# First tokens turned inside the routing steps, two whole weight quarters fetched ahead of them, row numbers written during the dense layers

## The chip, the cores and the metric

The kernel runs on one NeuronCore of a Trainium2 chip. A core has TensorE (PE: matmuls; PEld: its weight loads), VectorE (DVE), ScalarE (ACT), GpSimd (POOL) and SyncE (SP). Each takes its instructions in the order of the program and waits for semaphores of the others. Sixteen DMA engines move data between HBM and the on-chip memory; here SP issues nearly all transfers and POOL the gathers and the final scatter, which go by lists of row numbers. The metric is the device time of one execution in microseconds (us).

## The reference

Three stages, one behind the other, all in float32:

```python
x = attention(q, k, v)      # 2 x 8 heads x 768 x 64: a window of 16 on each side, and 24 block summaries
logits = x @ w_gate         # [1536, 8]
for idx in argsort(-logits.flatten()):          # greedy: the best (token, expert) pair first
    if token free and expert has fewer than 192 tokens: assign
out[mask_e] = relu(x[mask_e] @ w1[e]) @ w2[e]   # 8 experts of 192 tokens, 512 -> 1024 -> 512
h = out @ w_in; g = where(h >= 1, h, where(h <= -1, 0, (h + 1)**2 / 4))
result = g @ w_out          # 512 -> 2048 -> 512
```

## The kernel before

**Attention** (lines 103 to 404) is a list of small steps, written out by hand in ORDER (lines 53 to 100); each step issues on a fixed engine, so the list is the order of every engine's queue. Its last steps are `x_turn` (four transposes of 128 finished tokens, line 346), `x_out` (their copy out of PSUM), `logits` (eight matmuls with `w_gate`, line 357), `logits_out` (their copy into `lg`, line 130 on DVE) and `x_store` (the tokens to the DRAM tensor `xdram`, line 341).

**Routing** finds the greedy assignment in eight phases, one for each expert that fills. `scale` (line 478) reduces `lg` to its largest magnitude `m`, spreads it over the partitions with a transpose and a matmul (lines 484, 489), and finds with `best` (lines 506 to 514, five DVE operations) each token's best expert `oh`. A phase then makes five rounds (`first`, `mask`): DVE writes a mask `mk` (line 677), PE counts with twelve matmuls (line 565), DVE makes flags, PE spreads them with one matmul (line 575). PE and DVE take turns here, and each waits for the other. At the end of a phase the chosen expert's number `ei` is known (the step `expert`), and some steps on, its 192 row numbers `idx` (line 688, the step `places`).

**Experts.** `fetch` (line 711) gathers the 192 tokens of an expert in two halves of 96 rows (line 717, on POOL), and stores the row numbers to the DRAM tensor `idxd` (line 719, on SP). For the first expert SP also issues a tiny store `spare` of one gathered row (line 723): SP waits there until the second half has landed, and all later weight loads stand behind it. An expert's weights come as four quarters of 1 MB (`weights`, line 725): two of w1, two of w2. The first quarter of the first expert is cut in two halves (lines 744, 745), of which one stands ahead of the tokens. `transposed` (line 749) turns one half of the tokens on PE and copies it out on ACT; `mlp` (line 760) is a generator of 64 steps of one matmul each (lines 776, 785).

**What sets the order.** `run_experts` runs the routing generator; PLAN gives, for each of its turns, how much PE work of another kind is put in. While `turns` (counted from the first `places` on) is at most WAIT = 8, that is `idle(n)`: n matmuls on zeros (line 709) that compute nothing. After that it is n steps of the experts' products. The first of these turns both halves of the first tokens (`turn(0)`, with three idle matmuls ahead of each half).

**Dense layers.** `FeedForward.steps` makes 16 rounds (`s`) of seven products, takes weights as 64-bit `raw` tiles from SP, which DVE converts, and scatters results to rows `idxo`, which `run` reads back from `idxd` (line 1208) at its start.

**Pools.** Tiles come from pools. A pool opened on bytes of closed pools makes its tiles wait, by default, for every user of those pools, transfers included.

Of the kernel before, what the change touches and what calls it, by code (L numbers as in the profile page):

```python
# [36 lines left out]
2 5 2 1 2 2 2 2 2 2 2 2 2 1 10 10 3 3 3 3 3 2 4 2 2 2 2 9 9 2 3 3 3 3 3 3 3 3 2 2 16 9 3 3 3 3 3 3 3 3 3 2 2 10  # L37
# [3 lines left out]
WAIT = 8  # L41
# [56 lines left out]
logits_out 8 act; x_store 11; x_turn 11; pv_out 9 1; x_out 11 dve; x_turn 9; x_store 9; x_out 9 act; logits 11;  # L98
logits 9; logits_out 11 dve; logits_out 9 dve
# [3 lines left out]
def attention(tc, ctx, C, q, k, v, wg, xdram, lg, later, order=ORDER):  # L103
# [239 lines left out]
    def x_turn(t):  # L343
        p = live["xp", t] = ptr()
        for c in range(4):
            nc.tensor.transpose(p[:, c], live["x", t][:, c * 128:(c + 1) * 128], ident)  # L346
# [5 lines left out]
    def logits(t):  # L352
        p = live["l", t] = ptr()
        for c in range(4):
# [7 lines left out]
    def begin():  # L362
        warm = st.tile([128, 512], BF, name="warm")
# [43 lines left out]
class Router:  # L407
# [15 lines left out]
    def open(self, ctx):  # L423
        self.wk = ctx.enter_context(self.tc.tile_pool(name="rt_work", bufs=2, side="right"))
        self.pp = ctx.enter_context(self.tc.tile_pool(name="rt_psum", bufs=2, space=PSUM, side="right"))

    def consts(self):
# [27 lines left out]
        g.memset(self.ones, 1.0)  # L455
# [21 lines left out]

    def scale(self):
# [14 lines left out]
        r = wk.tile([128, 2], F32, name="r")  # L493
        nc.vector.tensor_scalar(r[:, 0:1], p[:, :1], 1.0 / (half - 0.25), 1e-36, op0=OP.mult, op1=OP.max)
        nc.vector.reciprocal(r[:, 1:2], r[:, 0:1])

        self.v0 = wk.tile([128, NT], F32, name="v0")
        nc.vector.tensor_scalar(self.v0, v, r[:, 1:2], half, op0=OP.mult, op1=OP.add)
        self.r = r
# [18 lines left out]
    def phase(self, k):  # L518
# [13 lines left out]
        if not last:  # L532
            oh = self.oh
            for j in range(LEVELS):
# [25 lines left out]
                if k == 0 and j == 0:  # L560
                    nc.vector.tensor_scalar(Z, self.lg, self.r[:, 1:2], KARY / 2, op0=OP.mult, op1=OP.add)
# [129 lines left out]
class Experts:  # L691


    def __init__(self, tc, ctx, C, xdram, w1, w2, router, ff, idxd, spare, xp):
        self.tc, self.nc, self.C, self.spare = tc, tc.nc, C, spare
        self.x, self.w1, self.w2, self.rt = xdram, w1, w2, router
        self.ff, self.idxd, self.xp = ff, idxd, xp
        self.quarters = 0
        self.post = []
        self.wk = ctx.enter_context(tc.tile_pool(name="ex_work", bufs=2))  # L700
        self.pp = ctx.enter_context(tc.tile_pool(name="ex_psum", bufs=2, space=PSUM))
# [9 lines left out]
    def fetch(self, k):  # L711
# [13 lines left out]
    def weights(self, k, j, q):  # L725
# [16 lines left out]
        if k == 0 and j == 0:  # L742

            q.dma_start(a[:, :, :256], src[:, :, :256])
            self.rest = lambda: q.dma_start(a[:, :, 256:], src[:, :, 256:])
        else:
            q.dma_start(a, src)
# [49 lines left out]
def run_experts(router, ex, ff, leave, plan=PLAN):  # L797
# [26 lines left out]
    def load():  # L824

        while loaded[0] < min(4 * known[0], room() if placed[0] else 1):
            k, j = divmod(loaded[0], 4)

            if loaded[0] == 1:
                ex.rest()  # L830
# [35 lines left out]
    for r in route():  # L866
# [10 lines left out]
        else:  # L877
            ex.idle(n)
    for n, _ in enumerate(run):
# [5 lines left out]
class FeedForward:  # L885
# [7 lines left out]
    def __init__(self, tc, ctx, C, w_in, w_out, idxd, out):  # L893
        self.tc, self.nc, self.ctx = tc, tc.nc, ctx
        self.w_in, self.w_out, self.idxd, self.out = w_in, w_out, idxd, out
# [202 lines left out]
    def early(self, spare):  # L1098

        nc, tc = self.nc, self.tc  # L1100
        self.wk = self.ctx.enter_context(tc.tile_pool(name="ff_work", bufs=2, side="right"))
        self.pp = self.ctx.enter_context(tc.tile_pool(name="ff_psum", bufs=2, space=PSUM, side="right"))
# [21 lines left out]
    def steps(self):  # L1124
# [74 lines left out]

    def run(self, ctx):  # L1200
        nc, tc = self.nc, self.tc
        self.ww = ctx.enter_context(tc.tile_pool(name="ff_split", bufs=3))
        self.op = ctx.enter_context(tc.tile_pool(name="ff_out", bufs=1, space=PSUM))
# [3 lines left out]
        idx = self.idx = self.st.tile([128, NT], I32, name="idxo")  # L1207
        nc.sync.dma_start(idx, bass.AP(tensor=self.idxd.tensor, offset=self.idxd.offset, ap=[[1, 128], [128, NT]]))
# [4 lines left out]
def build(tc, q, k, v, w_gate, w1, w2, w_in, w_out, out):  # L1213
    nc = tc.nc
    with ExitStack() as ctx:
# [17 lines left out]
        with ExitStack() as c1:  # L1233
            attention(tc, c1, C, q, k, v, wg, xdram, lg, (rt.consts, rt.consts2))
        ff = FeedForward(tc, ctx, C, w_in, w_out, idxd, out)
        c4 = ExitStack()
        xp = c4.enter_context(tc.tile_pool(name="ex_x", bufs=2, side="right"))
# [32 lines left out]
```

## Time and profile before

| | |
|---|---|
| median of the runs shown | 597.09 us (593.78, 597.09, 1673.16) |
| the profiled execution | 594.48 us |
| its span on the core | 592.4 us |
| PE busy | 569.9 us (96%) |
| DVE, ACT, POOL busy | 405.1, 276.4, 174.3 us |
| chain that ended last: PE, DVE, issue | 82%, 10%, 2% |

The 2.1 us between span and execution lie outside the core's instructions. In forty slices PE is at 9 tenths or more nearly everywhere from slice 9 on; slices 6 and 7 (89 to 118 us) hold the passage from attention to the experts. Busy there includes the idle matmuls on zeros, so the busy share alone does not show what work is done.

### The profile page before, as it was taken

Reading aid. Unit: us, or ns where it says so; the run is one execution under the profiler, and the core shown is the slowest. Engines: PE = TensorE matmul, PEld = TensorE weight load, DVE = VectorE, ACT = ScalarE, POOL = GpSimd, SP = SyncE. Lnnn points to the kernel's source line nnn. Section 1 sums busy time; section 2 is a strip of 40 time slices with the busy share of each in tenths; the row PEclk is TensorE's granted clock in tenths of the full one; section 3 lists DMA queues with packets and bytes.
Section 4 is the critical chain, followed back from the end, with each engine's and each line's share of the span. In section 5 each row is a group of like instructions: output and inputs, shape, how many; then the busy total and the mean of one; then the engine's idle time right before and its main releaser. Section 6 shows DMA issues by size and latency. Waiting matters only on the chain.

```text
span 592.4 us, 11433 instructions
## 1 busy us (share of the span) xinstructions
PE 569.9 (96%) x4298; PEld 485.2 (82%) x4298; DVE 405.1 (68%) x1092; ACT 276.4 (47%) x637; POOL 174.3 (29%) x271
## 2 busy tenths in 40 slices
PE   6799998999999999999999999999999999999996
PEld 4568683478988888899999988888888888989884
DVE  6887775753665755645666898886799886666651
ACT  5576670021222222223221756566677766666653
POOL 5412100100101101113000443333355875555424
PEclk9999998999999999999999999999999999999999
DMA  9999124388738659598888232100000100000002
GB/s 214 189 207 203 38 75 143 52 284 286 231 114 280 208 108 282 108 189 221 286 284 279 88 102 89 37 2 1 1 0 1 71 37 2 0 1 1 2 0 107
DMA packets 84073, 71.42 MB, mean 121 GB/s; under 512 B 42546, under 2 KB 71218, under 8 KB 84018
## 3 DMA queue, kind: packets, MB, share of 16 engines
q1 hardware_dynamic: 81506, 64.38, 39.8%
q0 software_dynamic: 1984, 6.29, 4.2%
q8 instruction: 34, 0.56, 0.4%
q14 instruction: 21, 0.17, 0.1%
q10 hardware_dynamic: 528, 0.02, 0.1%
HBM read 64.38 MB, written 6.30 MB: 119 GB/s over the span
## 4 chain that ended last, share of the span: by engine, by line
PE 82%; DVE 10%; issue 2%; ACT 2%; POOL 1%; DMA 1%; POOLq 0%; DVEq 0%; SPq 0%
PE po L1049 18%; PE ph L1016 17%; PE acc L776 15%; PE acc L785 14%; PE rt L565 2%; PE po L318 2%; PE pt L304 2%; PE px L709 2%; PE ps L280 1%; PE ptr L212 1%; DVE gl L1032 1%; DMA nat<-in_q_dram 1%; PE px L757 1%; PE ptr L346 1%; POOL out_dram L1067 1%
## 5 line engine op out<-in xcount | busy, mean ns | idle before, releaser
L776 PE MATMUL acc<-xt,slot 128*128 128x192 f32 x512 | 94.3, 333 | 0.6 <-ACT xt L758 0.6
L785 PE MATMUL acc<-ht,slot 128*128 128x192 f32 x512 | 94.2, 332 | 0.0
L776 PEld LDWEIGHTS acc<-xt,slot 128*128 128x128 f32 x512 | 82.3, 190 | 1.3 <-ACT xt L758 0.8
L785 PEld LDWEIGHTS acc<-ht,slot 128*128 128x128 f32 x512 | 82.5, 190 | 0.5
L994 POOL TENSOR_TENSOR al<-sums,ah 128x256 fp32r<-128x256 f32 x64 | 52.8, 827 | 89.4 <-ACT ah L993 79.9
L1016 PE MATMUL ph<-yh,ah 128*128 128x384 f32 x218 | 75.1, 344 | 1.7 <-DVE c L1119 1.1
L1049 PE MATMUL po<-wl,gh 128*128 128x512 f32 x192 | 76.0, 396 | 0.3 <-POOL wl L1007 0.3
L1049 PE MATMUL po<-wh,gl 128*128 128x512 f32 x192 | 75.9, 395 | 0.0
L1049 PE MATMUL po<-wh,gh 128*128 128x512 f32 x192 | 75.8, 395 | 0.0
L1016 PE MATMUL ph<-yl,ah 128*128 128x384 f32 x218 | 73.7, 338 | 0.0
L1016 PE MATMUL ph<-yh,al 128*128 128x384 f32 x218 | 73.6, 338 | 0.0
L717 POOL DMA_INDIRECT xg<-xdram,idx x16 | 15.0, 937 | 179.9 <-ACT idx L688 59.5
L994 POOL TENSOR_TENSOR al<-slot,ah 128x256 fp32r<-128x256 f32 x48 | 41.6, 867 | 79.0 <-PE ph L1016 43.0
L1029 ACT ACTIVATE gh<-u 128x384 fp32r<-128x384 f32 x64 | 33.4, 522 | 59.0 <-DVE u L1027 58.6
L1032 DVE TENSOR_TENSOR gl<-u,gh 128x384 fp32r<-128x384 f32 x64 | 51.3, 801 | 6.8 <-ACT gh L1029 6.7
L780 ACT ACTIVATE ht<-acc 128x192 f32<-128x192 f32 x64 | 21.0, 330 | 64.0 <-PE acc L776 64.0
L1016 PEld LDWEIGHTS ph<-yh,ah 128*128 128x128 f32 x218 | 40.9, 188 | 9.9 <-DVE u L1146 3.0
L1016 PEld LDWEIGHTS ph<-yl,ah 128*128 128x128 f32 x218 | 40.9, 188 | 3.9
L1049 PEld LDWEIGHTS po<-wl,gh 128*128 128x128 f32 x192 | 36.1, 188 | 6.1 <-POOL wl L1007 0.7
L1049 PEld LDWEIGHTS po<-wh,gl 128*128 128x128 f32 x192 | 36.1, 188 | 6.0
L1016 PEld LDWEIGHTS ph<-yh,al 128*128 128x128 f32 x218 | 40.9, 188 | 0.0
L790 ACT ACTIVATE yr<-acc 128x192 f32<-128x192 f32 x32 | 10.5, 330 | 64.5 <-PE acc L785 64.5
(228 smaller groups left out, 996.0 us busy)
## 6 DMA issues: line engine op xcount, KB each, us to landing
slot<-in_moe_w_dram SPq DMA_DIRECT2D x31, 1024.0 KB, 8.3
raw<-in_moe_w_in_dram SPq DMA_DIRECT2D x16, 512.0 KB, 5.4
raw<-in_moe_w_out_dram SPq DMA_DIRECT2D x16, 512.0 KB, 5.4
vw<-in_v_dram SPq DMA_DIRECT2D x20, 192.0 KB, 5.7
nat<-in_k_dram SPq DMA_DIRECT2D x12, 256.0 KB, 5.0
nat<-in_q_dram SPq DMA_DIRECT2D x12, 256.0 KB, 5.3
xdram<-xs SPq DMA_DIRECT2D x12, 256.0 KB, 2.9
slot<-in_moe_w_dram SPq DMA_DIRECT2D x2, 512.0 KB, 5.6
```

What stands on the lines that cost most here:

```text
L304: nc.tensor.transpose(pt[:, c], pr[:, c], ident)
L318: nc.tensor.matmul(po[64 * w:64 * w + 64, c], pt[:, c, 64 * w:64 * w + 64], VW[b * G + i // 2][:, n, 2 * c + a], start=True, stop=True)
L565: nc.tensor.matmul(p[:KARY, :E], mk[:, t], oh[:, t], start=(t == 0), stop=(t == NT - 1))
L717: nc.gpsimd.indirect_dma_start(out=self.XG[k][:, h], out_offset=None, in_=self.x, in_offset=bass.IndirectOffsetOnAxis(ap=idx[:, h:h + 1], ...
L776: nc.tensor.matmul(p, w[:, c, f % 4 * 128:f % 4 * 128 + 128], xt[:, c], start=(c == 0), stop=(c == 3))
L780: nc.scalar.activation(ht[:, f], p, AF.Relu)
L785: nc.tensor.matmul(p, w[:, f, c % 2 * 128:c % 2 * 128 + 128], ht[:, f], start=(f == 0), stop=(f == 7))
L994: nc.gpsimd.tensor_tensor(l, x, h.bitcast(F32), op=OP.subtract)
L1016: nc.tensor.matmul(p, w[:, 128 * c:128 * c + 128], y[:, b, c], start=first and n == 0, stop=n == 5, skip_group_check=True)
L1029: nc.scalar.activation(gh, u, AF.Copy)
L1032: nc.vector.tensor_tensor(gl, u, gh.bitcast(F32), op=OP.subtract)
L1049: nc.tensor.matmul(self.po[t], x[:, c], w, start=(self.left[t] == 6 * self.PAIRS - 1), stop=(self.left[t] == 0))
```

## The change

1. `reuse_waits="tile"` on the pools that are opened after attention (routing, experts, dense work): a tile waits only for earlier users of its own bytes.
2. `scale` is split: for the first 8 of 12 token tiles the five operations of `best` run inside attention's list (`later 2`), for the last 4 between the steps of `scale`; the scaling by a constant goes into the matmul (`ones` holds it, `tiny` keeps the sum above zero), so one DVE operation falls away.
3. Four matmuls on zeros (`unread`) in the last `x_turn` and `logits` steps.
4. Two whole quarters of the first expert's weights are loaded ahead of the `spare` store; the cut quarter is gone.
5. The two halves of the first tokens are turned at routing turns 5 and 6 (HALVES), without the idle matmuls; WAIT is 7, and PLAN is changed to suit.
6. The eight stores of row numbers leave `fetch`; a new `rows` issues them, and the read of `idxo`, in round 5 of the dense layers.

```diff
 PLAN = """
-2 5 2 1 2 2 2 2 2 2 2 2 2 1 10 10 3 3 3 3 3 2 4 2 2 2 2 9 9 2 3 3 3 3 3 3 3 3 2 2 16 9 3 3 3 3 3 3 3 3 3 2 2 10
+3 2 3 2 1 2 2 2 2 2 2 2 2 2 1 10 10 3 3 3 2 2 2 3 2 2 2 2 9 9 2 3 3 3 3 3 3 3 3 2 2 16 9 3 3 3 3 3 3 3 3 3 2 2 10
...
-WAIT = 8
+WAIT = 7
+HALVES = 5, 6
...
-logits_out 8 act; x_store 11; x_turn 11; pv_out 9 1; x_out 11 dve; x_turn 9; x_store 9; x_out 9 act; logits 11;
-logits 9; logits_out 11 dve; logits_out 9 dve
+logits_out 8 act; x_store 11; x_turn 11 1; pv_out 9 1; x_out 11 dve; later 2; x_turn 9 2; x_store 9; x_out 9 act; logits 11;
+logits 9 1; logits_out 11 dve; logits_out 9 dve
...
+    def unread(p, n):
+        for _ in range(n):
+            nc.tensor.matmul(p.rearrange("p a b -> p (a b)"), live["warm"][:, :128], live["warm"], start=True, stop=True)
...
-        self.wk = ctx.enter_context(self.tc.tile_pool(name="rt_work", bufs=2, side="right"))
+        self.wk = ctx.enter_context(self.tc.tile_pool(name="rt_work", bufs=2, side="right", reuse_waits="tile"))
...
     def scale(self):
 
         nc, wk, lg = self.nc, self.wk, self.lg
+        rest = list(self.first(slice(8, NT)))
         m = wk.tile([128, 1], F32, name="m")
         nc.vector.tensor_reduce(m, lg, axis=AX.XY, op=OP.max, apply_absolute_value=True)
+        yield "scale"
         p = self.ps()
         nc.tensor.transpose(p[:1, :128], m, self.C["ident"])
+        for o in rest[:2]:
+            o()
         yield "scale"
         m2 = wk.tile([1, 1], F32, name="m2")
         nc.vector.tensor_reduce(m2, p[:1, :128], axis=AX.X, op=OP.max)
         p = self.ps()
-        nc.tensor.matmul(p[:, :1], self.ones[:1], m2, start=True, stop=True)
+        nc.tensor.matmul(p[:, :1], self.ones, self.tiny, start=True, stop=False)
+        nc.tensor.matmul(p[:, :1], self.ones, m2, start=False, stop=True)
         yield "scale"
-        v = yield from self.best(lg)
+        for o in rest[2:]:
+            o()
...
-        nc.sync.dma_start(bass.AP(tensor=self.idxd.tensor, offset=self.idxd.offset + k // 4 * (N // 2) + k % 4 * 96,
-                                  ap=[[1, 96], [HALF, 2]]), idx)
...
-        while loaded[0] < min(4 * known[0], room() if placed[0] else 1):
+        while loaded[0] < min(4 * known[0], room() if placed[0] else 2):
...
-    def turn(k):
-        for h in range(2):
-            if k == 0:
-                ex.idle(3)
+    def turn(k, halves=(0, 1)):
+        for h in halves:
             ex.transposed(k, h)
-        turned[0] = k + 1
+        turned[0] = k + (halves[-1] == 1)
...
             ex.idle(n)
+            if turns in HALVES:
+                turn(0, (HALVES.index(turns),))
...
+            if s == P - 3:
+                self.rows()
...
+    def rows(self):
+
+        nc, d = self.nc, self.idxd
+        for k in range(E):
+            nc.sync.dma_start(bass.AP(tensor=d.tensor, offset=d.offset + k // 4 * (N // 2) + k % 4 * 96,
+                                      ap=[[1, 96], [HALF, 2]]), self.places[k])
+        self.idx = self.st.tile([128, NT], I32, name="idxo")
+        nc.sync.dma_start(self.idx, bass.AP(tensor=d.tensor, offset=d.offset, ap=[[1, 128], [128, NT]]))
```

How the change moves instructions is shown at three places. First DVE, from the last copies of `lg` to the first mask `mk`, before:

```order
L130 COPY xt<-ptr 128x512
L130 COPY lg<-ptr 128x8 x2
L482 TENSOR_REDUCE m<-lg 128x1
L487 TENSOR_REDUCE m_1712<-rt 1x1
L506 TENSOR_REDUCE v<-lg 128x12
...
L514 TENSOR_TENSOR oh<-w,mx 128x96
L494 TENSOR_SCALAR r<-rt 128x1
L495 RECIPROCAL r<-r 128x1
L498 TENSOR_SCALAR v_1734<-v,r 128x12
L540 TENSOR_SCALAR zi<-v_1734 128x24
L677 TENSOR_TENSOR mk<-zi,lev_500 128x384
```

and now:

```order
L131 COPY xt<-ptr 128x512
L501 TENSOR_REDUCE v0b<-lg 128x8
...
L131 COPY lg<-ptr 128x8 x2
L512 TENSOR_REDUCE m<-lg 128x1
L501 TENSOR_REDUCE v0b<-lg 128x4
L502 TENSOR_TENSOR w_1634<-lg,v0b 128x32
L520 TENSOR_REDUCE m_1733<-rt 1x1
...
L505 TENSOR_TENSOR oh_1636<-w_1634,mx_1635 128x32
L529 RECIPROCAL r<-rt 128x1
L532 TENSOR_SCALAR v_1747<-v0b,r 128x12
L574 TENSOR_SCALAR zi<-v_1747 128x24
L711 TENSOR_TENSOR mk<-zi,lev_500 128x384
```

Five operations on eight tiles of tokens stand ahead of the copies of `lg` now, two on the other four tiles between `m` and the maximum over partitions, three behind it, and one step of the scaling is gone.

Second PE, in the first expert's wait for its tokens (the second phase of the routing), before, from the flags of its fourth round on:

```order
L575 MATMUL rt<-fl,unit_508 128x2
L709 LDWEIGHTS blank
L709 MATMUL px<-blank 128x512
...
L757 MATMUL px<-ident,xg 128x96 x4
...
L757 MATMUL px<-ident,xg 128x96 x4
L776 MATMUL acc<-xt,slot_1671 128x192 x2
L565 LDWEIGHTS mk
L565 MATMUL rt<-oh,mk 32x8
```

and now, from the flags of its second round to its fourth count:

```order
L609 MATMUL rt<-fl,unit_506 128x2
...
L784 MATMUL px<-ident,xg 128x96 x4
L599 LDWEIGHTS mk
L599 MATMUL rt<-oh,mk 32x8
...
L784 MATMUL px<-ident,xg 128x96 x4
L609 MATMUL rt<-fl,unit_507 128x2
...
L599 MATMUL rt<-oh,mk 32x8
L803 MATMUL acc<-xt,slot_1686 128x192 x3
```

The first half of the tokens (`xg`) is turned ahead of the third count, the second half ahead of the third round's flags, and the first product (`acc`) follows the fourth count; before, both halves and the first product stood between the fourth flags and the fifth count.

Third SP's queue around the first tokens (`slot` is a weight quarter, `spare` the store that waits for the tokens, `ISA` sets an address), before:

```order
L729 TENSOR_LOAD ei
L729 ISA x2
L744 ISA
L744 DMA slot_1671<-in_moe_w_dram 128x4x256
L719 DMA idxd<-idx_1990 96x2x1
L723 DMA spare<-xg 1x8
L745 ISA
L745 DMA slot_1671<-in_moe_w_dram 128x4x256
L747 ISA
L747 DMA slot_1672<-in_moe_w_dram 128x4x512
```

and now:

```order
L761 TENSOR_LOAD ei
L761 ISA x2
L774 ISA
L774 DMA slot_1686<-in_moe_w_dram 128x4x512
L774 ISA
L774 DMA slot_1687<-in_moe_w_dram 128x4x512
L755 DMA spare<-xg 1x8
L774 ISA
L774 DMA slot_1688<-in_moe_w_dram 128x8x256
```

Ahead of the tokens stand 2 MB instead of half a megabyte, and the store of the row numbers is gone from between.

## Rows read from the trace of the kernel before

**Rows 1.** Stretches: length, then PE, PEld, DVE, ACT, POOL busy; clock, DMA, GB/s.

```profile
145.00:330.00 185.00, 183.19 (x1364) 170.04 (x1363) 111.78 (x427) 47.38 (x133) 19.20 (x23) 1.00 0.72 210
330.00:350.00 20.00, 19.09 (x103) 17.31 (x102) 18.48 (x30) 11.23 (x28) 9.20 (x9) 1.00 0.37 106
```

**Rows 2.** Timeline, end of attention to first count: start, length, what [idle before <-releaser].

```profile
92.02 0.17 DVE L130 COPY lg<-ptr 128x8 f32<-128x8 f32 x1 [0.65 <-PE ptr L357]
92.63 0.25 DVE L482 TENSOR_REDUCE m<-lg 128x1 f32<-128x96 f32 x1 [0.45 <-DMA xdram<-xs]
93.63 0.38 PE L489 MATMUL rt<-m,ones 1*128 1x1 f32 x2
93.94 1.68 PE L709 MATMUL px<-blank 128*128 128x512 bf16 x7
94.66 0.26 DVE L514 TENSOR_TENSOR oh<-w,mx 128x96 bf16<-128x96 bf16 x1
96.11 0.46 PE L565 MATMUL rt<-oh,mk 128*32 128x8 bf16 x12 [0.49 <-DVE mk L677]
```

**Rows 3.** Second phase, timeline: third count, landed tokens, second turning, first product, fifth count.

```profile
117.42 0.46 PE L565 MATMUL rt<-oh,mk 128*32 128x8 bf16 x12
120.62 0.30 SPq L723 DMA_DIRECT2D spare<-xg  x1
122.59 0.55 PE L757 MATMUL px<-ident,xg 96*128 96x96 f32 x4
123.72 0.92 PE L776 MATMUL acc<-xt,slot 128*128 128x192 f32 x4 [0.58 <-ACT xt L758]
124.57 0.46 PE L565 MATMUL rt<-oh,mk 128*32 128x8 bf16 x12
```

**Rows 4.** First phase: timeline, fourth and fifth count; then two stretches as in rows 1.

```profile
102.40 0.46 PE L565 MATMUL rt<-oh,mk 128*32 128x8 bf16 x12
104.16 0.46 PE L565 MATMUL rt<-oh,mk 128*32 128x8 bf16 x12
...
96.00:106.00 10.00, 9.22 (x85) 3.56 (x85) 5.59 (x36) 0.00 (x0) 0.00 (x0) 0.83 0.10 40
99.00:100.00 1.00, 1.00 (x5) 0.16 (x5) 0.79 (x4) 0.00 (x0) 0.00 (x0) 0.50 0.00 0
```

**Rows 5.** Row numbers and first gathers, timeline; last line: first gather, issue to landing.

```profile
110.80 0.17 ACT L688 ACTIVATE idx<-rt 96x2 int32<-96x2 f32 x1 [3.66 <-PE rt L686]
111.84 1.15 POOL L717 DMA_INDIRECT xg<-xdram,idx  x1 [42.63 <-DVE v L506]
113.29 0.92 POOL L717 DMA_INDIRECT xg<-xdram,idx  x1 [0.30 <-issue]
...
DMA to landing us min/median/max: 8.0/8.0/8.0
```

**Rows 6.** Gathers of the second and of the last expert, issue to landing.

```profile
DMA to landing us min/median/max: 5.7/6.5/7.4
...
DMA to landing us min/median/max: 12.6/12.8/13.0
```

**Rows 7.** From the chain in order of time: 64 records of products back to back.

```profile
287.63 10.40 PE acc L776 x64
```

**Rows 8.** Weights, issue to landing: first half quarter, other half, whole quarters (from the page).

```profile
DMA to landing us min/median/max: 7.7/7.7/7.7
...
DMA to landing us min/median/max: 3.4/3.4/3.4
...
slot<-in_moe_w_dram SPq DMA_DIRECT2D x31, 1024.0 KB, 8.3
```

**Rows 9.** Last raw loads (SP's timeline), first scatter, stores of row numbers (page).

```profile
367.21 10.75 SPq L925 DMA_DIRECT2D raw<-in_moe_w_out_dram  x2
...
L1067 POOL DMA_INDIRECT out_dram<-slot,idxo x12: 968/972/1097, 464.6 to 587.7; - x12
...
idxd<-idx SPq DMA_DIRECT2D x8, 0.8 KB, 13.0
```

More of the change, by code (lines that the diff above doesn't have):

```diff
@@ L350, in x_out, with logits @@
         evac(eng, xt, live.pop(("xp", t)))
-    def logits(t):
+    def logits(t, blanks=0):
         p = live["l", t] = ptr()
+        unread(p, blanks)
         for c in range(4):
@@ L362, in begin @@
     def begin():
[L363 removed]
+        warm = live["warm"] = st.tile([128, 512], BF, name="warm")
         nc.vector.memset(warm, 0.0)
@@ L423, in open @@
     def open(self, ctx):
-        self.wk = ctx.enter_context(self.tc.tile_pool(name="rt_work", bufs=2, side="right"))
-        self.pp = ctx.enter_context(self.tc.tile_pool(name="rt_psum", bufs=2, space=PSUM, side="right"))
+        self.wk = ctx.enter_context(self.tc.tile_pool(name="rt_work", bufs=2, side="right", reuse_waits="tile"))
+        self.pp = ctx.enter_context(self.tc.tile_pool(name="rt_psum", bufs=2, space=PSUM, side="right", reuse_waits="tile"))
     def consts(self):
@@ L454, in consts @@
         self.ones = st.tile([1, 128], F32, name="ones")
-        g.memset(self.ones, 1.0)
+        g.memset(self.ones, 1.0 / (KARY / 2 - 0.25))
+        self.tiny = st.tile([1, 1], F32, name="tiny")
+        g.memset(self.tiny, 2.0e-35)
         self.left = st.tile([128, E], F32, name="left")
@@ L476, in ps, with ahead, first @@
         return self.pp.tile([128, 512], F32, name="rt")
+    def ahead(self):
+        st, full = self.st, [128, NT, E]
+        self.best0 = [st.tile(s, d, name=n) for n, s, d in (("v0b", [128, NT], F32), ("w0", full, BF),
+                                                            ("mx0", [128, NT], F32), ("oh0", full, BF))]
+        for o in self.first(slice(0, 8)):
+            o()
+    def first(self, s):
+        nc, lg = self.nc, self.lg
+        v, w, mx, oh = (a[:, s] for a in self.best0)
+        full = [128, s.stop - s.start, E]
+        z, rev = lg[:, s], self.rev[:, None, :].to_broadcast(full)
+        yield lambda: nc.vector.tensor_reduce(v, z, axis=AX.X, op=OP.max)
+        yield lambda: nc.vector.tensor_tensor(w, z, v[:, :, None].to_broadcast(full), op=OP.is_equal)
+        yield lambda: nc.vector.tensor_tensor(w, w, rev, op=OP.mult)
+        yield lambda: nc.vector.tensor_reduce(mx, w, axis=AX.X, op=OP.max)
+        yield lambda: nc.vector.tensor_tensor(oh, w, mx[:, :, None].to_broadcast(full), op=OP.is_equal)
     def scale(self):
         nc, wk, lg = self.nc, self.wk, self.lg
+        rest = list(self.first(slice(8, NT)))
         m = wk.tile([128, 1], F32, name="m")
         nc.vector.tensor_reduce(m, lg, axis=AX.XY, op=OP.max, apply_absolute_value=True)
+        yield "scale"
         p = self.ps()
         nc.tensor.transpose(p[:1, :128], m, self.C["ident"])
+        for o in rest[:2]:
+            o()
         yield "scale"
@@ L691, with __init__ @@
 class Experts:
[L694 removed]
+    def __init__(self, tc, ctx, C, xdram, w1, w2, router, ff, spare, xp):
         self.tc, self.nc, self.C, self.spare = tc, tc.nc, C, spare
         self.x, self.w1, self.w2, self.rt = xdram, w1, w2, router
[L697 removed]
+        self.ff, self.xp = ff, xp
         self.quarters = 0
         self.post = []
[L700 to L701 removed]
+        self.wk = ctx.enter_context(tc.tile_pool(name="ex_work", bufs=2, reuse_waits="tile"))
+        self.pp = ctx.enter_context(tc.tile_pool(name="ex_psum", bufs=2, space=PSUM, reuse_waits="tile"))
         self.W, self.XG, self.XT, self.number = {}, {}, {}, {}
@@ L741, in weights @@
         self.W[k, j] = a
[L742 to L747, printed above, removed]
+        q.dma_start(a, src)
     def transposed(self, k, h):
@@ L1100, in early @@
         nc, tc = self.nc, self.tc
-        self.wk = self.ctx.enter_context(tc.tile_pool(name="ff_work", bufs=2, side="right"))
-        self.pp = self.ctx.enter_context(tc.tile_pool(name="ff_psum", bufs=2, space=PSUM, side="right"))
+        self.wk = self.ctx.enter_context(tc.tile_pool(name="ff_work", bufs=2, side="right", reuse_waits="tile"))
+        self.pp = self.ctx.enter_context(tc.tile_pool(name="ff_psum", bufs=2, space=PSUM, side="right", reuse_waits="tile"))
         self.half = self.st.tile([128, 1], F32, name="half")
@@ L1233, in build @@
         with ExitStack() as c1:
-            attention(tc, c1, C, q, k, v, wg, xdram, lg, (rt.consts, rt.consts2))
-        ff = FeedForward(tc, ctx, C, w_in, w_out, idxd, out)
+            attention(tc, c1, C, q, k, v, wg, xdram, lg, (rt.consts, rt.consts2, rt.ahead))
+        ff = FeedForward(tc, ctx, C, w_in, w_out, idxd, out, rt.idx)
         c4 = ExitStack()
-        xp = c4.enter_context(tc.tile_pool(name="ex_x", bufs=2, side="right"))
+        xp = c4.enter_context(tc.tile_pool(name="ex_x", bufs=2, side="right", reuse_waits="tile"))
         rt.open(c4)
         with ExitStack() as c2:
-            ex = Experts(tc, c2, C, xdram, w1, w2, rt, ff, idxd, spare, xp)
+            ex = Experts(tc, c2, C, xdram, w1, w2, rt, ff, spare, xp)
             run_experts(rt, ex, ff, c4.close)
```

27 lines of the change are left out of this document (12 added, 15 removed).

## The prediction

> **What bounds the kernel now.** I read first the busy shares by stretch. From 145 to 330 us PE is busy 183.19 of 185 us [rows 1]: once the experts' products run, PE is full, and no transfer or other engine can give anything back there. The dense stage is as full; only its first 20 us show a gap, 0.9 us [rows 1]. So this change can act in one place: the passage from the last `lg` (92.2 us) to the first product (123.72 us) [rows 2, 3], 31.5 us in which PE runs the routing's small matmuls and zeros. Each us by which the products start earlier moves all that follows by a us, since the same PE work stands behind them.
>
> In the timeline of the passage there are two limits in turn. Up to the row numbers it is the ping-pong of PE and DVE. After that it is the landing of the tokens: SP's store that waits for them runs at 120.62, both halves are turned by 123.1, the first product starts at 123.72 [rows 3].
>
> **Front of the routing (parts 1 to 3).** Before, `m` waits 0.45 us for a token store [rows 2]; now it waits for `lg` alone. But the zeros cost: one of them takes (1.68 - 0.38) / 6 = 0.22 us, with 0.38 the length of a single one, as 7 in a row take 1.68 [rows 2], and the one ahead of the last `logits` needs the PSUM buffer that `x_out` frees, so it can't run early. `lg` is done at 92.19 + 0.22 + 0.05 = 92.46 instead of 92.19, and `m` starts at 92.48 instead of 92.63. From `m` to the end of the matmul that spreads it took 1.4 us [rows 2]; with the `tiny` matmul it ends at about 94.0. Before, the five operations on all tokens held DVE until 94.92, and the first count came 1.2 us later, at 96.11 [rows 2]. Now three small ones (0.26 each, bounded by `oh` in [rows 2]) run behind the maximum, at about 93.45 to 94.25, and the count stands 1.2 us later, at 95.45: **0.7 us** gained. The five early ones cost nothing where DVE waits anyway: it is idle 0.65 us ahead of the last copy of `lg` [rows 2] and before that. If that cover fails, their 1.3 us push `lg` back by up to 0.6. Bounds: 0.1 (zeros and early operations both delay) to 1.1 (neither does).
>
> **Clock in the first phase.** The five counts take 96.11 to 104.16, 8.05 us, and the last cycle 1.76 [rows 2, 4]. Over 96 to 106 the granted clock was 0.83, and 0.50, the lower level of 1.2 GHz, in the middle [rows 4]. PE had been idle in pieces before that: 0.45 us of DVE's wait, then the wait for the mask. At the full clock the four cycles take some 4 x 1.76 = 7.0, so 1.0 us is there to gain. The four new zeros and the shorter wait leave fewer gaps, and I take **0.9** (bounds 0 and 1.0). Together the row numbers come 1.6 us earlier, and the gathers start at 111.84 - 1.6 = 110.24 and 111.69 [rows 5].
>
> **Landing of the first tokens (parts 4 to 6).** The first gather landed 8.0 us after its start [rows 5]; the second expert's took 5.7 and 7.4 in the middle of streaming weights, the last expert's 12.6 to 13.0 [rows 6]. Now 2 MB instead of half a megabyte stand ahead, and the store of 192 single numbers is gone. The nearest row is the second expert's, with heavy weight traffic beside it: I take 7.0 for both, so they land at 117.25 and 118.7. Bounds 5.7 and 13.0.
>
> The third count was at 117.42 [rows 3], so the routing could run it at 115.8 now; but the turning of the first half stands ahead of it on PE, and PE waits until 117.25. The turning takes 0.55 to 0.6 [rows 3]: third count at 117.95. The cycle of 1.76 with the second turning of 0.6 in it (landed 118.7, just in time) puts the fourth count at 120.3, and the first product 0.46 later at **120.77**, against 123.72: 2.95 earlier. Behind the waiting PE stand only routing and zeros; DVE waits with it.
>
> Not all of that is gain, for the fifth count is still to come. A step of products is 2 records, 10.40 / 32 = 0.325 us [rows 7]. Now five steps (1.63), the flags' matmul (0.17) and a gap of about 0.2 stand between 120.77 and the fifth count at 122.77; before it stood at 124.57 with two steps done [rows 3]. So 1.8 us earlier and three steps (0.98) further: **2.8 us**, with bounds 0.9 (no clock gain, gathers as slow as 8.0) and 4.7 (5.7 us, all of the front). Weights don't hold it: two quarters issued side by side ahead of the row numbers (109.2 now), at 8.3 [rows 8], land by about 117.5; the third quarter, behind the store at 118.8, has until the 33rd step, over 10 us later.
>
> **Other waits and the stores.** At the start of the dense stage finer waits may free part of the 0.9 us gap [rows 1]: **0.2** (0 to 0.9; a changed order could also cost as much). The eight stores leave SP's queue among the weights, where PE was not waiting [rows 1]: 0. In their new place SP reaches them after the last raw load, near 378, and the scatter needs them at 464.6 [rows 9], so 86 us cover eight stores and the read. Each landed in 13.0 [rows 9]; issued in a row they overlap.
>
> **Sum**, on the profiled execution's own 594.48 us: 594.48 - 2.8 - 0.2 = **591.5 us**. The two other runs without the outlier are 593.78 and 597.09, so that execution is 2.6 below the median of the runs shown; by that median the sum would say 594.1.
>
> **A rule against it.** The trace shows the first gather at 8.0 us with 512 KB and a store of numbers ahead of it, and one at 5.7 to 7.4 with quarters in flight [rows 5, 6]. The Trainium skill (DMA: Bandwidth & Descriptors, section Queues, rings and completion order) says that a transfer's semaphore is written only after every earlier write of that DMA engine, across its queues. By that rule the tokens would not count as landed before the two quarters have; the gathers at 12.6 to 13.0 would fit that, those at 5.7 to 7.4 speak against a long hold. By the rows the sum stays at 591.5; by the rule alone it stays there too if the quarters land by 117.5, and goes the way of the first rival below, up to 597.6, if they land later than the tokens would.
>
> **Rivals.**
> - *Tokens held behind the two quarters (slower).* For it: half a quarter took 7.7 us to land here, although the other half took 3.4 [rows 8]; and gathers took 13.0 [rows 6]. Against it: the 5.7 to 7.4 among streaming weights. At 13.0 the second half lands at 124.7; turning, the rest of the cycle and a count put the first product at about 126.7, 3.0 later than before: with the accounting above about 3.1 lost, **597.6 us**. It decides from a second landing later than some 9.7 us after its start.
> - *The clock falls in the new wait.* PE now stands idle some 1.5 us ahead of the first turning, where it ran zeros before. The stretch of 0.83 means 2 x 0.17 x 10 = 3.4 us at the lower level [rows 4]; if that comes over the first products, half of it is lost, 1.7: **593.2**.
> - *The first phase keeps its low clock.* The gain of 0.9 falls away: **592.4**.
> - *Tokens land at 5.7* [rows 6]: at 115.95 and 117.4, so third count 116.6, fourth 119.0, product 119.4, 1.4 better: **590.1**.
> - *Row numbers too late.* If the eight stores went strictly one behind the other at 13.0, they and the read would end near 378 + 104 + 5 = 487, 22 us after the first scatter wants them, and POOL's later work stands behind it: about **613**, over 2% slower. Against it: the 31 quarters of 8.3 us would take 257 one behind the other [rows 8], and all of them land between 109 and 330, so transfers on this queue overlap. It decides from 10 us each.
>
> **How the numbers follow.** Forecast 0.42; fast tokens 0.15; low clock in the first phase 0.14; clock in the wait 0.14; late tokens 0.11; late row numbers 0.02; anything else 0.02. The range takes in all but the late tokens and row numbers: the lower end is the best of all bounds, 594.48 - 4.7 - 0.9 = 588.9, with 0.7 for runs below the profiled one, 588.2; the upper end 593.2 with 2.6 for runs above it, 595.8. Two per cent, about what a measurement of this kernel can tell from no change, is 11.9 us; only the late row numbers or something unseen reach it: faster 0.02, same 0.95, slower 0.03.
>
> **What would show it.** In the profile after: `m` following the copy of `lg` with no wait on a store, and first count near 95.5; granted clock 1.00 from 95 to 105; gathers landing about 7 us after their start, PE idle 1 to 2 us ahead of the first turning; first product near 120.8; a span near 589.4. A second landing past 121.4, or a clock of 0.50 between 117 and 124, would make it wrong.

## The result, and the profile after

The changed kernel takes 589.26 us (588.67 to 590.3), the kernel before on the same chip 594.36 us (the median of six, one outlier of 1673.16 us among them): a ratio of 0.991, interval 0.989 to 0.994. The profiled execution has a span of 586.8 us, 5.6 less than before.

Timeline of the changed kernel, end of attention to the counts of the first phase (start, length, engine, line, what):

```profile
91.71 0.17 DVE L131 COPY lg<-ptr 128x8 f32<-128x8 f32 x1 [0.63 <-PE ptr L364]
91.98 0.25 DVE L512 TENSOR_REDUCE m<-lg 128x1 f32<-128x96 f32 x1
94.66 0.46 PE L599 MATMUL rt<-oh,mk 128*32 128x8 bf16 x12
...
101.78 0.46 PE L599 MATMUL rt<-oh,mk 128*32 128x8 bf16 x12
```

`m` no longer waits for a store; from it to the first count pass 2.68 us, against 3.48 [rows 2]. The five counts take 7.12 us, against 8.05 [rows 2, 4]. The stretch of this phase (as in rows 1: PE, PEld, DVE, ACT, POOL busy, clock, DMA, GB/s) has the full clock, where rows 4 have 0.83:

```profile
96.00:106.00 10.00, 9.07 (x82) 3.79 (x81) 6.68 (x42) 0.38 (x1) 0.00 (x0) 1.00 0.04 16
```

The timeline from the row numbers to the fifth count of the second phase, and the two gathers from issue to landing:

```profile
108.42 0.17 ACT L722 ACTIVATE idx<-rt 96x2 int32<-96x2 f32 x1 [3.72 <-PE rt L720]
109.46 1.14 POOL L751 DMA_INDIRECT xg<-xdram,idx  x1 [40.81 <-DVE v L540]
110.91 0.92 POOL L751 DMA_INDIRECT xg<-xdram,idx  x1 [0.30 <-issue]
114.95 0.52 PE L784 MATMUL px<-ident,xg 96*128 96x96 f32 x4
115.36 0.31 SPq L755 DMA_DIRECT2D spare<-xg  x1
115.40 0.46 PE L599 MATMUL rt<-oh,mk 128*32 128x8 bf16 x12
116.23 0.49 PE L784 MATMUL px<-ident,xg 96*128 96x96 f32 x4
117.50 0.46 PE L599 MATMUL rt<-oh,mk 128*32 128x8 bf16 x12
117.88 1.24 PE L803 MATMUL acc<-xt,slot 128*128 128x192 f32 x6
120.01 0.46 PE L599 MATMUL rt<-oh,mk 128*32 128x8 bf16 x12
```

```profile
DMA to landing us min/median/max: 4.4/4.9/5.4
```

The tokens land at 114.9 and 115.3, the halves are turned on either side of the third count (115.40), and the first product starts at 117.88, 5.84 earlier than in [rows 3]. Of these, 2.38 come from the earlier row numbers (108.42 against 110.80 [rows 5]; 0.93 of that is a low clock in the trace of the kernel before, see "Late stores alone"), and 3.46 from the landing and the turning behind it. The fifth count comes 4.56 earlier, with three more steps of products done (0.98): 5.5 us, nearly all of the span's 5.6. Behind it nothing else is gained: PE is as full while the products run, and the start of the dense layers still has its gap [rows 1].

```profile
145.00:330.00 185.00, 183.81 (x1358) 171.60 (x1357) 117.20 (x426) 50.38 (x140) 23.44 (x26) 1.00 0.64 210
330.00:350.00 20.00, 19.13 (x95) 16.66 (x94) 19.40 (x32) 11.73 (x27) 9.43 (x9) 1.00 0.42 132
```

### The profile page after: what moved, and what is told of

Read it like the earlier page. It is cut to its first block, busy times and chain, and to the rows that moved or that the text cites. A ratio compares the mean times of both kernels' runs of the same rounds, so it can differ in the third digit from the quotient of the medians.

```text
span 586.8 us, 11408 instructions
## 1 busy us (share of the span) xinstructions
PE 568.0 (97%) x4293; PEld 484.9 (83%) x4293; DVE 407.4 (69%) x1096; ACT 276.2 (47%) x637; POOL 176.3 (30%) x272
## 4 chain that ended last, share of the span: by engine, by line
PE 82%; DVE 10%; ACT 3%; issue 2%; POOL 1%; POOLq 0%; DVEq 0%; ACTq 0%
PE po L1073 17%; PE ph L1040 17%; PE acc L803 15%; PE acc L812 14%; PE rt L599 2%; PE po L319 2%; PE pt L305 2%; PE ps L281 2%; PE px L743 1%; ACT kw L129 1%; DVE gl L1056 1%; PE ptr L352 1%; PE px L784 1%; PE ptr L174 1%; PE ptr L364 1%
## 5 line engine op out<-in xcount | busy, mean ns | idle before, releaser
L817 ACT ACTIVATE yr<-acc 128x192 f32<-128x192 f32 x32 | 10.5, 329 | 63.9 <-PE acc L812 63.9
```

## Experiments

The theory after the result: the tokens landed sooner than forecast because the store of row numbers had gone from beside the gathers, and the early turning made time of that. Its rivals: the loads ahead set the landing, or the front of the routing and its clock carry the gain. Diffs are against the changed kernel, unless another is named; ratios are to the kernel before.

**The stores put back among the weights.** The eight stores stand in `fetch` again, and `rows` only reads.

```diff
+        d = self.ff.idxd
+        nc.sync.dma_start(bass.AP(tensor=d.tensor, offset=d.offset + k // 4 * (N // 2) + k % 4 * 96,
+                                  ap=[[1, 96], [HALF, 2]]), idx)
         if k == 0:
```

> The changed kernel with part 6 undone: each expert's 192 row numbers are stored where the tokens are fetched again. Theory A (the store of single numbers holds up the gather that stands beside it): the first gathers land 7 to 8 us after their start instead of 5.4 and 4.4, the first product comes about 2.3 us later, near 120.2 instead of 117.9, and the time is some 2 us over the changed kernel's (ratio to before about 0.9945 instead of 0.9912). Theory B (the gather was slow before for another reason, for instance weights that came in two pieces): landing 5.4 and 4.4 as now, no change of time, ratio 0.991.

Measured: 598.26 us, ratio 1.007 (1.004 to 1.010), so slower than before. Store, first turning and first products in the timeline; the landing of the store and of the two gathers; stretches around the wait:

```profile
108.52 0.34 SPq L754 DMA_DIRECT2D idxd<-idx  x1
120.68 0.87 PE L787 MATMUL px<-ident,xg 96*128 96x96 f32 x4 [5.87 <-DMA xg<-xdram,idx]
124.99 2.29 PE L806 MATMUL acc<-xt,slot 128*128 128x192 f32 x6
```

```profile
DMA to landing us min/median/max: 11.8/11.8/11.8
...
DMA to landing us min/median/max: 9.9/10.6/11.2
```

```profile
115.00:118.00 3.00, 0.00 (x0) 0.00 (x0) 0.17 (x1) 0.00 (x0) 0.00 (x0) 1.00 0.07 3
...
121.00:124.00 3.00, 3.00 (x24) 1.79 (x23) 0.57 (x5) 0.88 (x2) 0.00 (x0) 0.50 0.52 74
124.00:127.00 3.00, 3.00 (x20) 2.18 (x18) 0.86 (x6) 0.10 (x1) 0.00 (x0) 0.50 1.04 292
```

The store lands at 108.52 + 11.8 = 120.3 and the gathers at 120.6 and 120.7, some 5.5 us later than in the changed kernel. No weights are behind that, for the DMA engines move 3 GB/s from 115 to 118. Nor is it the tokens' own data: both halves (0.39 MB, on the gathers' queue `q0`) have moved by 115.5, and the store's numbers have gone out by 114 (first line: all packets from 113 to 114, 234 of them under 512 bytes; second: `q0` from 113 to 115.5, packets and MB).

```profile
DMA packets 354, 0.36 MB, mean 363 GB/s; under 512 B 234, under 2 KB 234, under 8 KB 354
...
q0 software_dynamic: 128, 0.39, 55.6%
```

PE idles 5.87 us and then works at 0.50, the lower level of 1.2 GHz, from 121 to 127 and somewhat longer, over the first products (the first six matmuls take 2.29 us instead of 1.24). So the store holds the tokens, at a far higher price than expected: 9 us, the late landing and the clock together.

**Half a quarter ahead, and four quarters.** The first cuts the first quarter again, as before, so that 0.5 MB stand ahead of the tokens; the second puts 4 MB there.

```diff
-        while loaded[0] < min(4 * known[0], room() if placed[0] else 2):
+        while loaded[0] < min(4 * known[0], room() if placed[0] else 1):
             k, j = divmod(loaded[0], 4)
+            if loaded[0] == 1:
+                ex.rest()
```

> The changed kernel with part 4 undone: half a quarter of weights ahead of the tokens, the rest behind them. Theory A: the gathers land at 4.4 to 5.4 us as in the changed kernel or a little sooner, since nothing else moves; but the second half of the first quarter and the second quarter are issued only at about 115.9, land 3.4 and some 6 us later, and the products want them from the 9th step (about 120.5) and the 17th (about 124): a stall of 0 to 1 us, ratio 0.991 to 0.993. Theory B (two whole quarters are what lets the tokens land early): landing back at 7 to 8, ratio about 0.9945.

```diff
-        while loaded[0] < min(4 * known[0], room() if placed[0] else 2):
+        while loaded[0] < min(4 * known[0], room() if placed[0] else 4):
```

> The changed kernel with four quarters (4 MB) of weights ahead of the tokens instead of two. If a gather's landing waits for all transfers that stand ahead of it on the same engines, the tokens land when 4 MB have moved at the 390 to 410 GB/s seen with two, about 107.5 + 10.5 = 118 and a little more, 3 us later than now, and the first product moves by as much: ratio about 0.9965. If the gather only shares the engines (round robin), it lands 1 to 2 us later than now, some 6 to 7 us after its start, and the time rises by 0 to 1.5 us: ratio 0.991 to 0.9935.

Measured: 589.3 us, ratio 0.991 (0.988 to 0.994), and 590.43 us, ratio 0.993 (0.990 to 0.995). The token store, the first product and the first expert's two gathers, of the first kernel and then of the second:

```profile
114.02 0.31 SPq L755 DMA_DIRECT2D spare<-xg  x1
117.68 1.24 PE L808 MATMUL acc<-xt,slot 128*128 128x192 f32 x6
...
DMA to landing us min/median/max: 3.0/3.2/3.3
```

```profile
119.52 1.24 PE L803 MATMUL acc<-xt,slot 128*128 128x192 f32 x6
...
DMA to landing us min/median/max: 6.2/6.4/6.5
```

Loads ahead do slow the gathers: the second lands after 3.0, 4.4 and 6.5 us with 0.5, 2 and 4 MB ahead. But they share the engines and do not hold: with 4 MB ahead the tokens land at 117.7, while weights move at 325 to 348 GB/s until past 119. Part 4 is worth nothing that shows; without it the tokens come 1.3 us sooner, and the first product 0.2, since the counts stand between.

**Late stores alone, on the kernel before.** Part 6 without the rest: the store leaves `fetch`, and `rows` is called at `s == P - 3`.

```diff
-        nc.sync.dma_start(bass.AP(tensor=self.idxd.tensor, offset=self.idxd.offset + k // 4 * (N // 2) + k % 4 * 96,
-                                  ap=[[1, 96], [HALF, 2]]), idx)
...
+            if s == P - 3:
+                self.rows()
```

> The kernel before with part 6 alone: its row numbers are stored in the dense layers. Theory A: its first gathers land at about 5 us instead of 8.0 and 7.3. Theory B: they land as before. In both the time hardly moves (ratio 0.997 to 1.000), since PE reaches the turning of the tokens by its own order of work only at 121.3, 0.7 us after they had landed anyway.

Measured: 595.91 us, ratio 1.002 (1.000 to 1.003). The gathers and the first product:

```profile
DMA to landing us min/median/max: 3.1/3.1/3.2
```

```profile
122.83 0.92 PE L774 MATMUL acc<-xt,slot 128*128 128x192 f32 x4 [0.58 <-ACT xt L756]
```

The store alone cost the first gather 4.8 us: 3.2 against 8.0 [rows 5]. The tokens are there at 115.6, 5 us sooner than [rows 3], and nothing is gained by it, since PE's order keeps the turning behind the fourth count. Early tokens are worth nothing without part 5. (The first product is 0.89 earlier than in [rows 3], which is the clock, below.)

The same trace answers two more questions. First the gathers of the second and of the last expert, now without their stores:

```profile
DMA to landing us min/median/max: 6.3/7.3/8.2
...
DMA to landing us min/median/max: 5.8/6.0/6.2
```

The second expert's are no faster than with the store (5.7 and 7.4 [rows 6]): in the kernel before, that store was issued at 136.6, 4.4 us behind the first of the two gathers, and landed 9 us after the second. The last expert's take 5.8 to 6.2 instead of 12.6 to 13.0 [rows 6]; there the store had been issued 5.5 us ahead of them.

Second the clock of the first phase. The front of the routing is the kernel before's here, and so are PE's waits in it, ahead of the transpose of `m` and of the first count (first line before; then of this kernel the two waits, the fifth count and the stretch):

```profile
92.99 0.27 PE L484 MATMUL rt<-ident,m 128*1 128x128 f32 x1 [1.01 <-DVE m L482]
```

```profile
93.02 0.27 PE L484 MATMUL rt<-ident,m 128*1 128x128 f32 x1 [1.03 <-DVE m L482]
96.14 0.46 PE L565 MATMUL rt<-oh,mk 128*32 128x8 bf16 x12 [0.49 <-DVE mk L677]
103.26 0.46 PE L565 MATMUL rt<-oh,mk 128*32 128x8 bf16 x12
...
96.00:106.00 10.00, 8.72 (x88) 3.78 (x89) 6.42 (x41) 0.15 (x1) 0.00 (x0) 1.00 0.06 23
```

The granted clock is 1.00 all the same, the five counts take 7.12 us as in the changed kernel, and the row numbers come at 109.90, 0.90 earlier than 110.80 [rows 5]. So the low clock of [rows 4] belongs to that execution: the kernel before can run this phase at the full clock without any of the front's changes.

**The turns as before.** Part 5 undone in the changed kernel (both halves at the first product turn, with three idle matmuls ahead of each).

```diff
-WAIT = 7
-HALVES = 5, 6
+WAIT = 8
+HALVES = ()
...
+            if k == 0:
+                ex.idle(3)
             ex.transposed(k, h)
```

> The changed kernel with part 5 undone: the plan of before, WAIT = 8, both halves of the first tokens turned in the first turn of the products with zeros ahead of each. If the early turning is what uses the early tokens, the first product goes back to about 6.3 us after the third count, near 121.4 instead of 117.9, and net of the three steps some 3.2 us are lost: ratio to before near 0.9965. Rival: the early row numbers alone carry the gain, and less than 1 us is lost, ratio under 0.993.

Measured: 593.08 us, ratio 0.997 (0.996 to 0.999). The tokens have landed by 115.50, the first product waits until 121.32:

```profile
115.50 0.31 SPq L755 DMA_DIRECT2D spare<-xg  x1
121.32 0.92 PE L803 MATMUL acc<-xt,slot 128*128 128x192 f32 x4 [0.58 <-ACT xt L785]
```

Parts 5 and 6 need each other: 5 without 6 loses 0.7%, 6 without 5 gains nothing, and undoing 5 alone takes 0.6 of the 0.9% away. The front of the routing can carry no more than what is left.

**The front, part by part.** Three kernels undo one piece each: the pools' `reuse_waits="tile"` taken away everywhere (part 1); the four zeros taken out of attention's list (part 3); all five operations of `best` on all twelve tiles put behind `lg` (the early half of part 2).

```diff
-        self.wk = ctx.enter_context(self.tc.tile_pool(name="rt_work", bufs=2, side="right", reuse_waits="tile"))
+        self.wk = ctx.enter_context(self.tc.tile_pool(name="rt_work", bufs=2, side="right"))
```

> The changed kernel with part 1 undone: tiles wait for every user of the pools whose bytes they take. The first reduction waits for the last token store again, as before (0.45 us there). Expected: the first count 0.3 to 0.6 us later and the time with it, ratio 0.992. Rival: the waits at the start of the dense layers are worth as much again, ratio 0.993.

```diff
-logits_out 8 act; x_store 11; x_turn 11 1; pv_out 9 1; x_out 11 dve; later 2; x_turn 9 2; x_store 9; x_out 9 act; logits 11;
-logits 9 1; logits_out 11 dve; logits_out 9 dve
+logits_out 8 act; x_store 11; x_turn 11; pv_out 9 1; x_out 11 dve; later 2; x_turn 9; x_store 9; x_out 9 act; logits 11;
+logits 9; logits_out 11 dve; logits_out 9 dve
```

> The changed kernel with part 3 undone: no matmuls on zeros in the last steps of attention. If they hold the clock, the granted clock falls to 0.50 for some 3 us in the first phase again, its four cycles take 8.0 us instead of 7.1, and the time rises by about 0.8 us (0.9 less 0.1 for the zeros that no longer delay the last logits): ratio 0.9925. Rival: the shorter waits behind attention suffice for the clock, and the time falls by 0.1 to 0.3: ratio 0.991.

```diff
-        rest = list(self.first(slice(8, NT)))
+        rest = list(self.first(slice(0, NT)))
...
-        for o in rest[:2]:
-            o()
         yield "scale"
...
-        for o in rest[2:]:
+        for o in rest:
             o()
```

> The changed kernel with the early part of part 2 undone: the five operations that find each token's best expert run on all 12 tiles behind the maximum, none in attention's list. Expected: DVE holds the first count up by 0.5 to 0.8 us, ratio 0.992 to 0.9925; if the gap on PE also lowers the clock in the first phase, 0.9 us more, ratio 0.994. Rival: nothing, since they ran beside the matmuls before: ratio 0.991.

Measured: 589.15 us, ratio 0.991 (0.990 to 0.993); 588.77 us, ratio 0.990 (0.989 to 0.991); 590.02 us, ratio 0.992 (0.991 to 0.994). None differs measurably from the changed kernel. Their traces, in this order (for the second, a copy in attention and the last copy of `lg`):

```profile
92.11 0.25 DVE L512 TENSOR_REDUCE m<-lg 128x1 f32<-128x96 f32 x1 [0.21 <-DVE lg L131]
```

```profile
50.26 1.09 ACT L129 ACTIVATE kw<-ptr 128x512 f32<-128x512 f32 x2 [0.54 <-PE ptr L213]
...
91.74 0.17 DVE L131 COPY lg<-ptr 128x8 f32<-128x8 f32 x1 [0.39 <-PE ptr L364]
```

```profile
95.20 0.46 PE L599 MATMUL rt<-oh,mk 128*32 128x8 bf16 x12 [0.52 <-DVE mk L711]
```

With the pools' whole waits `m` starts 0.13 later and the first count (94.97) 0.31; with `best` late the first count comes 0.54 later. Without the zeros the last `lg` comes 41.48 us after the copy in attention, with them 91.71 - 49.98 = 41.73: they cost 0.25. The clock from 96 to 106 is 1.00 without the zeros and with `best` late too, as it is with the whole front of before ("Late stores alone"). All twelve traces of the changed kernel and its variants have 1.00 there, and of the two with the front of before one has; whether the change makes the low clock rarer is open.

**What makes so small a store slow.** First the changed kernel with a store of half as many numbers, 96, beside the first gathers.

```diff
         if k == 0:
+            d = self.ff.idxd
+            nc.sync.dma_start(bass.AP(tensor=d.tensor, offset=d.offset, ap=[[1, 96], [HALF, 1]]), idx[:, 0:1])
```

> The changed kernel with one more store beside the first gathers: 96 single numbers (half of the first expert's) go to the DRAM tensor of row numbers, which the late stores write again. In the kernel with all stores among the weights, a store of 192 numbers took 11.8 us to land and both gathers landed within 0.4 us after it, at 120.6 and 120.7. If the time is by the number of writes, 96 land in about 6 us, near 114.6, and the tokens at 115 to 116, hardly later than in the changed kernel (114.9 and 115.3): ratio 0.991 to 0.992. If any small store holds the tokens for a fixed time, they land near 120 again and the ratio is about 1.005.

Measured: 598.74 us, ratio 1.006 (1.004 to 1.008):

```profile
108.90 0.36 SPq L755 DMA_DIRECT2D idxd<-idx  x1
119.44 0.55 PE L786 MATMUL px<-ident,xg 96*128 96x96 f32 x4 [3.77 <-DMA xg<-xdram,idx]
```

Half the numbers hold the tokens nearly as long, until 119.4, 10.5 us from the store's start. These 96 numbers lie side by side in 384 bytes of HBM; the 192 of a whole store lie in two such pieces. So the last kernel keeps the 96 writes and moves them apart, each to a row of its own, 2 KB from the next.

```diff
         if k == 0:
+            nc.sync.dma_start(self.ff.far[:, 0:1], idx[:, 0:1])
...
+        ff.far = dp.tile([96, 512], I32, name="far")
```

> The changed kernel, with a store of the same 96 single numbers beside the first gathers as in e9_half_of_one_store, but each number goes to a row of its own, 2 KB from the next, in a tensor that nothing reads; e9 wrote them side by side into 384 bytes. The output is complete. If the store is slow because its 96 writes of 4 bytes meet in the same few hundred bytes of HBM (each write reads and writes back a block that the one before it is still writing), the writes are free of each other here: the tokens land 3 to 6 us after the gathers' start as in the changed kernel, first product near 118 us, ratio 0.990 to 0.993. If any store of single numbers with gathers and weights around it holds the gathers, wherever it writes, they land after 9 to 11 us, PE is idle for some 4 to 6 us, first product near 123 to 125 us, ratio 1.004 to 1.009. In between (landing near 7 to 8 us, first product near 120 to 121, ratio 0.996 to 1.000) both would have a part.

Measured: 589.13 us, ratio 0.990 (0.986 to 0.993), as without a store. Its timeline, and the landing of the gathers:

```profile
108.57 0.35 SPq L754 DMA_DIRECT2D far<-idx  x1
115.05 0.52 PE L785 MATMUL px<-ident,xg 96*128 96x96 f32 x4 [0.19 <-DMA xg<-xdram,idx]
117.98 1.24 PE L804 MATMUL acc<-xt,slot 128*128 128x192 f32 x6
```

```profile
DMA to landing us min/median/max: 4.5/5.0/5.5
```

It is where the numbers go that counts, not that they are single: 96 writes of 4 bytes into the same 384 bytes make the first turning 4.4 us later than the same writes 2 KB apart (119.44 against 115.05), and these leave it where it is without a store (114.95). The two kernels differ in the tensor as well, for `far` is one of its own; no kernel wrote 96 numbers side by side into such a tensor, so closeness was not tried apart from that.

**Products one turn earlier, and tokens sooner as well.** Two tries to gain more: `WAIT = 6`, and the same with half a quarter ahead and `HALVES = 4, 5`.

```diff
-WAIT = 7
-HALVES = 5, 6
+WAIT = 6
+HALVES = 4, 5
```

> The changed kernel with WAIT = 6: products start at the seventh turn, ahead of the fourth count, instead of two zeros there. The tokens are turned and copied by 117.26. PE waits up to 0.4 us for the copy and then does two steps (0.65) where zeros stood: 0.2 to 0.6 us won, ratio 0.990 to 0.991. Rival: the wait holds up the fourth count and with it the routing, and nothing is won: ratio 0.9912.

> Half a quarter of weights ahead of the tokens (as in the run with part 4 undone, where the tokens landed at 113.9 at the latest), the halves turned at turns 4 and 5 and the products from turn 7 on (WAIT = 6). The turning at turn 4 stands near 113.4 and waits up to 0.6 us; at turn 5 the second half is there. The first product starts ahead of the fourth count, near 116.6, about 1.2 us earlier than in the changed kernel: ratio 0.989 to 0.990. Rival: the second quarter, issued at 114.5 behind the tokens, lands too late for the 17th step or the wait at turn 4 holds up the routing, and nothing is won: ratio 0.991 or more.

Measured: 588.59 us, ratio 0.990 (0.988 to 0.992), and 588.38 us, ratio 0.988 (0.986 to 0.991). The first product starts at 117.42 and 117.10 instead of 117.88. Both may beat the changed kernel by some tenths of a us, but the intervals overlap; a gain is not shown.

## Why the prediction was right

Forecast were 591.5 us and no difference above 2%; it came to 589.26, inside the range (588.2 to 595.8) and near its lower end. The mechanism held: tokens that land earlier and are turned between the counts bring the products forward, and all that follows with them. The sizes held less well. Of the 5.5 us at the fifth count, 0.55 were unforeseen and 0.93 are not shown to be the change's; what is left for the landing and the early turning is 5.5 - 2.4 = 3.1, where 2.8 - 1.6 = 1.2 was forecast. By its steps:

- **What bounds the kernel** was right: PE was full after the passage, before and after, and the gain is there by the fifth count of the second phase; only 0.55 of it comes from ahead of the passage (below).
- **Front of the routing**: 0.7 forecast, 0.9 measured. The first count came 1.45 earlier (94.66 against 96.11 [rows 2]), of which 0.55 is attention's (below). The zeros cost 0.25, as forecast (0.27); the wait ahead of `m` that fell away and the steps from `m` to the count (2.68 us instead of 3.48) gave the rest.
- **Clock in the first phase**: 0.9 forecast, 0.93 measured, with 1.00 for 0.83, and this was luck. The forecast took the low clock of one trace for a property of the kernel, which fewer gaps on PE would mend. The kernel before with late stores alone has the same gaps (1.03 and 0.49 us) and 1.00, and the changed kernel without zeros has 1.00 too. So two executions with the same front differ by as much as was counted as a gain, and no run shows that the change brought it. The 0.45 us that the forecast names there as PE's idle time is DVE's wait; PE stood idle 1.01 us. The rival of a low clock did not come.
- **An unforeseen 0.55**: attention itself is earlier in the profiled execution. The difference is there at 50 us already, where both kernels have had the same instructions (first line before, second after):

```profile
50.53 1.09 ACT L128 ACTIVATE kw<-ptr 128x512 f32<-128x512 f32 x2 [0.55 <-PE ptr L212]
```

```profile
49.98 1.08 ACT L129 ACTIVATE kw<-ptr 128x512 f32<-128x512 f32 x2 [0.55 <-PE ptr L213]
```

  Late stores on the kernel before gave 50.54; all twelve traces of the changed kernel and its variants lie between 49.87 and 50.26. Nothing was tried on its cause; with it, 0.55 + 0.9 + 0.93 make the 2.38 by which the row numbers came earlier.
- **Landing of the first tokens** is the term that was mis-sized: 7.0 taken, 5.4 and 4.4 measured, so the likeliest rival (5.7) was the nearer. The row chosen as nearest, the second expert's [rows 6], stands among quarters in flight, and with or without a store its gathers take 5.7 to 8.2; ahead of the first tokens stand only 2 MB. The slow rows of that trace, 8.0 and the last expert's 12.6 to 13.0, were the stores': without them they are 3.2 and 5.8 to 6.2. So the step "the eight stores leave SP's queue among the weights, where PE was not waiting: 0" failed too. PE was not waiting for the stores, but gathers were.
- **The early turning**: with the tokens earlier, PE has almost no wait ahead of the first turning, where 1 to 2 us were forecast; the first product came at 117.88 instead of 120.77, and the net at the fifth count was 5.5 instead of 2.8, of which 0.55 is attention's. So the clock had no new wait to fall in. That rival is real all the same: with the store put back PE idles 5.87 us and then runs at 0.50.
- **Tokens held behind two quarters** did not come about. With 4 MB ahead the two gathers take 6.2 and 6.5 us, not 13.0.
- **The dense start**: 0.2 forecast, nothing gained (19.13 busy of 20, against 19.09).
- **The stores in their new place**: right, in the trace of the changed kernel they go out between 371.7 and 377.9, the read of `idxo` at 386.8, and the scatter starts at 458.7 (line, durations in ns, first and last start).

```profile
L1230 SPq DMA_DIRECT2D idxd<-idx x8: 304/436/449, 371.7 to 377.9; - x8
...
L1091 POOL DMA_INDIRECT out_dram<-slot,idxo x12: 967/970/1093, 458.7 to 582.0; - x12
```

The rule brought against the change fits the first experiment, with another transfer in the part of the late one: the tokens' data had moved by 115.5, and the gathers counted as landed at 120.6 and 120.7, with the store (120.3) and with the DMA engines idle meanwhile. The Trainium skill (DMA: Bandwidth & Descriptors, section Queues, rings and completion order) has a semaphore written only after every earlier write of that engine; the trace agrees for that store. Not every row is so simple. In the kernel before, the first expert's store landed at 117.8 and the gathers at 119.8 and 120.5, with their data still moving to the end (127 GB/s from 119 to 120). Its third store was issued 0.25 us ahead of the gathers and held nothing, for it landed at 171.4 and they at 162.9 and 164.1; most of its numbers went out only after the first of them (packets under 512 bytes: 49 from 155.7 to 162.9, 249 from there to 168). For the loads the rows show only a sharing of the engines.

## What to carry to other kernels

Before a wait for a transfer is priced by another row of the same kind, see what else stands in the queues ahead of both; a small store that nobody waits for can be what a large gather waits for. A transfer that comes earlier is worth only what the order of the waiting engine lets it use, so move both together and test each alone. Write small results late, or spread out in HBM as the kernel with `far` does, when something urgent is in flight. And before a low clock in one trace is counted as something to gain, look at a second execution.

## What the runs showed of the hardware

- 96 numbers of 4 bytes stored side by side into 384 bytes of HBM held gathers issued behind them until 10.5 us after the store's start, while the same numbers 2 KB apart, in a tensor of their own, left the gathers at 4.5 to 5.5 us from their own. With 192 numbers in two pieces of 384 bytes it was some 12 us. These go out within a us (in the kernel with all stores among the weights between 113 and 114); what passes from there to the landing at 120.3 is not shown.
- With 0.5 MB of weights ahead (the kernel before) the same store landed 6.8 us after its start, with 2 MB 11.8. The loads make it begin later: with 0.5 MB its numbers went out from 111.5 on, half a us after its start, and with 2 MB from 113 on, 4.5 us after it. From there both took some 6 to 7 us.
- A gather of 96 rows of 2 KB lands in 3.0 to 3.3 us with 0.5 MB of loads ahead of it, and in 6.2 to 6.5 with 4 MB.
- The same steps with the same waits on PE (1.01 and 0.49 us, 1.03 and 0.49) ran at a granted clock of 0.83 over 96 to 106 us in one execution, 0.50 in its middle, and of 1.00 in another.
